# Transposed blocks of the third and fourth unit moved by pairs of tiles: one write and two reads in place of two writes and four reads

## The chip, the cores and the metric

The kernel runs on one core of one Trainium2 chip. The metric is the device time of one execution in microseconds; the time given is the median of several executions of the same program. A profile of one further execution is read here. Its engines are PE (TensorE matmul), PEld (TensorE's loading of weights, which runs beside PE), DVE (VectorE), ACT (ScalarE), POOL (GpSimd) and SP (SyncE, which here only issues DMAs). Every DMA of this kernel is issued by SP, in the order of its program.

## The reference

Chunked attention over 8 x 8 heads with sequences of 576 in chunks of 64, then a maxout layer with three weight matrices and an output projection:

```python
scores = scale * np.matmul(q_c, k_c.transpose(0, 1, 2, 4, 3))      # 64 x 64 for each head and chunk
scores = scores - np.max(scores, axis=-1, keepdims=True)
attn = np.exp(scores)
attn = attn / (np.sum(attn, axis=-1, keepdims=True) + 1e-09)
out = np.matmul(attn, v_c)
...
x = np.ascontiguousarray(attn_out.transpose(0, 2, 1, 3)).reshape(B * S, H * D)   # 4608 x 512
h = np.maximum(np.maximum(x @ w1, x @ w2), x @ w3)                               # 512 -> 768
return (h @ w_out).astype(np.float32)                                            # 768 -> 512
```

All of it is float32. A product of float32 operands is made on TensorE from three products of split operands (high and low part), so each step of the maxout layer is three matmuls, on lines 187, 188 and 189.

## The kernel before, in words

The 4608 rows are 36 tiles of 128 rows. The first 8 tiles form two plain groups of four. The other 28 form four "units" of 6, 8, 8 and 6 tiles (`UNITS`), for which the maxout layer is computed with fewer products from mixed operands. A unit runs nine "sets" of products, and then a projection. A set reads one mixed weight matrix from a ring of two places in on-chip memory. The ring is filled from DRAM in three parts for each set (line 557): two of 128 x 1536 elements (768 KB) and one of 128 x 512 (256 KB). The first part is needed by the first product of a set, the second part by the second product, the third part only during the next set. A product is six matmuls. In the third unit a matmul has 512 columns, in the fourth 384.

While the products of one unit run, the attention of the next unit's tiles is put between them, pair of tiles by pair of tiles. `insertion` gives each step of a pair a due time on an estimated clock, and `passed` issues every step whose time has come. So the order on each engine's queue is settled when the program is built. For one tile the steps are: load of q and k (line 225) and of v (229), scores S (237), maximum, subtraction, exponential, sum, reciprocal, normalisation on POOL (204), a transposition of the attention weights, and the products with the values, V (296). V of a pair stands on PE's queue just ahead of S of the pair after it.

The transposition differs by unit. In the first groups and the first two units it is made by PE and copied by ACT (`transpose`, `transposed`). In the third and fourth unit (`PAIR_D`; seven pairs) it is made of 32 x 32 blocks by DVE (`blocks`, line 270, tile `xs`), and the blocks are put in their places by a trip through DRAM: for each tile one write (`to_scratch`, line 274, 256 KB) and two reads of 64 partitions (`from_scratch`, line 279, 128 KB each) into the tile `e`. The due times are in `PAIR_D`: the blocks of the two tiles at 7.6 and 9.5, the writes at 8.4 and 10.3, the reads at 13.2 and 14.4. SP waits in its own program for whatever a DMA needs before it issues it: for the DVE's blocks ahead of a write, and for the landing of the write ahead of a read. Everything behind it on SP's queue waits too, the parts of the weight ring among it.

The buffers: `xs` is a pool of two places, `e` has two places by the parity of the tile.

Of the kernel before, what the change touches and what calls it, by code (L numbers as in the profile page):

```python
# [9 lines left out]
F32 = mybir.dt.float32  # L10
# [10 lines left out]
P = 128  # L21
# [9 lines left out]
PAIR = (("mx", 1.4, 2.9), ("sub", 2.2, 3.7), ("exp", 3.1, 4.6), ("sum", 4.1, 6.0), ("eps", 5.0, 6.9), ("rec", 5.2, 7.1),  # L31
        ("nrm", 5.6, 7.5))
PAIR_T = (("T", 10.8, 13.0, 0.46), ("at", 11.4, 13.7, 0.0))
PAIR_D = (("bt", 7.6, 9.5, 0.0), ("bw", 8.4, 10.3, 0.0), ("br", 13.2, 14.4, 0.0))
OUT = (1, 2, 6, 7, 5, 4, 3)
MIX = 0.5

# [26 lines left out]
def chunk_attn_maxout_kernel(  # L64
# [10 lines left out]
    nc = tc.nc  # L75
# [3 lines left out]
    pad = pad_p.tile([P, 224], F32, name="pad")  # L79
    cpool = ctx.enter_context(tc.tile_pool(name="cpool", bufs=1))  # L80
    att = ctx.enter_context(tc.tile_pool(name="att", bufs=1))
    xs_p = ctx.enter_context(tc.tile_pool(name="xs_p", bufs=2))
    ep = ctx.enter_context(tc.tile_pool(name="ep", bufs=1))
    ao_p = ctx.enter_context(tc.tile_pool(name="ao_p", bufs=1))
    stage_p = ctx.enter_context(tc.tile_pool(name="stage_p", bufs=1))
    dram = ctx.enter_context(tc.tile_pool(name="dram", bufs=1, space=bass.MemoryType.DRAM))
# [40 lines left out]
    for name in FIRST.split():  # L127
        k = (3 * int(name[1]) + int(name[2])) if name[0] in "WAXY" else None
# [79 lines left out]
    halves_of = [slice(0, 64), slice(64, 128)]  # L208
# [3 lines left out]
    def bank_of(name):  # L212
        if name not in banks_of:
            banks_of[name] = ps[name].tile([P, 2, 2, 4, 64], F32, name=name[-1])
        return banks_of[name]

    def plain_steps(t, x_of, col):


        st = {}  # L220
# [21 lines left out]
            nc.vector.tensor_reduce(out=st["mx"].rearrange("p (g c) -> p c g", c=2), in_=st["s"], axis=AX.X, op=ALU.max)  # L242

        def less():
            st["e"] = ep.tile([P, 4, 2, 64], F32, name="e", tag=("et", "e")[t % 2])
            most = st["mx"].rearrange("p (g c) -> p c g", c=2)
            nc.vector.tensor_tensor(out=st["e"].rearrange("p g c k -> p c g k"), in0=st["s"],  # L247
                                    in1=most.unsqueeze(3).broadcast_to([P, 2, 4, 64]), op=ALU.subtract)
# [12 lines left out]
                                    identity=ident)  # L261

        def transposed():
            st["at"] = xs_p.tile([P, 4, P], F32, name="xs")
            nc.scalar.copy(out=st["at"], in_=st["tp"])

        def blocks():
            st["b"] = xs_p.tile([P, 4, 4, 32], F32, name="xs")
            for c in range(2):
                nc.vector.transpose(out=st["b"][:, 2 * c:2 * c + 2], in_=st["e"][:, :, c].rearrange("p g (k two) -> p two g k", two=2))  # L270

        def to_scratch():
            st["d"] = dram.tile([2, P, 2 * P], F32, name=f"b{t}")
            nc.sync.dma_start(out=st["d"].rearrange("c p x -> p c x"), in_=st["b"].rearrange("p (c j) g x -> p c (j g x)", c=2))

        def from_scratch():
            st["at"] = ep.tile([P, 4, 4, 32], F32, name="e", tag=("et", "e")[t % 2])
            for c, rows in enumerate(halves_of):
                nc.sync.dma_start(out=st["at"][rows].rearrange("p i g x -> p i (g x)"),
                                  in_=st["d"][c].rearrange("(i k) (j x) -> (k j) i x", i=4, j=2))  # L280

        def moving(a, g, b):
            if "d" in st:
                return st["at"][a, b.start // 32:b.stop // 32, g, :]
            return st["at"][a, g, b]

        def values():
# [21 lines left out]
        def pair(both):  # L309
# [1 line left out]

        return dict(q=load_qk, v=load_v, pair=pair, S=scores, mx=maximum, sub=less, exp=exp, sum=total,
                    eps=lambda: st["guard"](), rec=lambda: st["invert"](), nrm=lambda *eng: st["norm"](*eng),
                    T=transpose, at=transposed, bt=blocks, bw=to_scratch, br=from_scratch, V=values, xh=high, xl=low)

    begun = {}

# [515 lines left out]
    def plan(at, pe, fn):  # L833
        heapq.heappush(due, (at, len(order), pe, fn))
        order.append(fn)
# [15 lines left out]
    def next_load(u, k):  # L851
# [6 lines left out]
        s=lambda: hold("s", lambda: late["hold"].tile([P, 5, HALF], F32, name="kept")),  # L858
# [3 lines left out]
    g = moe(starts[1], lambda: x_tiles(1))  # L862
# [5 lines left out]
    pairs = []  # L868
    for u, (_, t0, count) in enumerate(units):
        for n in range(0, count, 2):  # L870
            both = dict(col=n * P, norm=nc.gpsimd if u else nc.vector, turn=PAIR_D if u > 1 else PAIR_T)
            both["tiles"] = [begun[t] if t in begun else plain_steps(t, stage, (t - t0) * P) for t in (t0 + n, t0 + n + 1)]
# [17 lines left out]
    def insertion(when, k, behind=0.0, apart=1.0):  # L890

        scored = pairs[k]["tiles"] if k < len(pairs) else []
        if k:
            plan(when, 0.0, value_banks(pairs[k - 1]))
            for n, steps in enumerate(pairs[k - 1]["tiles"]):
                plan(when + 0.001 * (n + 1), 0.5, steps["V"])
                plan(when + 1.2 + 0.6 * n, 0.0, staged(pairs[k - 1], n))
        lead = 1.0 * bool(k)
        for n, steps in enumerate(scored):
            plan(when + 0.003 + 0.001 * n, 0.65, steps["S"])  # L900
            for name, *at in PAIR:
                fn = steps[name]
                plan(when + lead + at[n], 0.0, (lambda fn=fn: fn(pairs[k]["norm"])) if name == "nrm" else fn)
            for name, *at, pe in pairs[k]["turn"]:
                plan(when + lead + behind + at[n], pe, steps[name])
            plan(when + 6.0 + apart * n, 0.0, steps["v"])
        if k + 1 < len(pairs):
            for n, steps in enumerate(pairs[k + 1]["tiles"]):
                plan(when + 4.0 + apart * n, 0.0, steps["q"])
# [112 lines left out]
```

## Time and profile before

| | us |
|---|---|
| median of 3 runs | 608.79 (608.75 to 609.01) |
| profiled execution, its own time | 608.11 |
| its span, first instruction to last | 606.3 |
| PE busy | 598.4 (99% of the span) |
| DVE busy | 421.9 (70%) |
| ACT busy | 290.0 (48%) |
| POOL busy | 187.3 (31%) |
| DMA engines' mean share | 69.6% (the queue that carries the kernel's own DMAs) |

A matmul is pipelined: the next begins before it ends, so PE's busy time is not the sum of its instructions. "Idle before" of an instruction is the time its engine stood still ahead of it, with the instruction or DMA that ended the wait. The chain of waits starts from the last instruction and goes back to what released each step. For a DMA, "to landing" is the time from its issue on SP to the arrival of all its data. The pairs of the third unit have their V at 281.7, 305.7, 329.7 and 353.7 us, those of the fourth at 405.0, 439.8 and 474.7 us.

### The profile page before, as it was taken

What the parts mean: (1) busy time and instruction counts of PE and PEld (TensorE: products, weight loads), DVE (VectorE), ACT (ScalarE), POOL (GpSimd) and SP (SyncE); (2) the same over time, 40 slices, a digit from 0 to 9 for tenths busy, and PEclk for the clock granted to TensorE, in tenths of its full rate; (3) what the DMA queues carried; (4) which work ended last, traced back from release to release, by engine and by line L of the source; (5) the groups of instructions that cost most, each with busy time, mean ns of one, the idle gap of its engine ahead of it and who ended that gap; (6) DMA issues with size and microseconds to landing.
All of it is one profiled execution on the core that took longest, in us unless ns stands there. A gap on an engine that the chain in (4) does not pass through costs nothing.

```text
span 606.3 us, 12703 instructions
## 1 busy us (share of the span) xinstructions
PE 598.4 (99%) x5045; PEld 520.7 (86%) x5046; DVE 421.9 (70%) x700; ACT 290.0 (48%) x522; POOL 187.3 (31%) x168
## 2 busy tenths in 40 slices
PE   8899999999999999999999999999999999999997
PEld 4888878888899999998888888888888888999997
DVE  5898965767987986895664669936374587344373
ACT  4887634433454554555243345642333364433353
POOL 3422577877232424100250622002424000131300
PEclk9999999999999999999999999999999999999999
DMA  8988667755868998748886894468657444677532
GB/s 346 369 311 268 254 191 282 291 187 231 309 238 321 359 340 300 256 141 284 278 280 234 283 356 161 161 232 290 232 199 267 151 156 128 223 260 259 189 130 79
DMA packets 59483, 148.95 MB, mean 246 GB/s; under 512 B 5664, under 2 KB 24608, under 8 KB 59424
## 3 DMA queue, kind: packets, MB, share of 16 engines
q1 hardware_dynamic: 59424, 148.13, 69.6%
q8 instruction: 40, 0.66, 0.4%
q14 instruction: 19, 0.16, 0.1%
HBM read 116.92 MB, written 31.20 MB: 244 GB/s over the span
## 4 chain that ended last, share of the span: by engine, by line
PE 96%; DVE 2%; ACT 1%; issue 0%; DVEq 0%
PE pm L187 30%; PE pm L188 29%; PE pm L189 29%; PE s L237 3%; PE pm L296 3%; PE tp L260 1%; PE pm L795 1%; DVE e L247 0%; DVE sm L195 0%; DVE xl L307 0%; PE s L296 0%; DVE mx L242 0%; DVE sm L198 0%; ACT e L251 0%; DVE ao L172 0%
## 5 line engine op out<-in xcount | busy, mean ns | idle before, releaser
L187 PE MATMUL pm<-X,ring 128*128 128x512 f32 (+1 forms) x504 | 184.4, 366 | 0.0
L189 PE MATMUL pm<-X,ring 128*128 128x512 f32 (+1 forms) x504 | 182.4, 362 | 0.0
L188 PE MATMUL pm<-X,ring 128*128 128x512 f32 (+1 forms) x504 | 182.4, 362 | 0.0
L626 ACT COPY kept<-pm 128x384 f32<-128x384 f32 (+1 forms) x144 | 76.7, 534 | 153.0 <-PE pm L189 152.8
L187 PEld LDWEIGHTS pm<-X,ring 128*128 128x128 f32 x504 | 94.6, 188 | 10.8 <-ACT kept L626 0.4
L189 PEld LDWEIGHTS pm<-X,ring 128*128 128x128 f32 x504 | 94.6, 188 | 9.9
L188 PEld LDWEIGHTS pm<-X,ring 128*128 128x128 f32 x504 | 94.7, 188 | 9.7
L632 POOL TENSOR_TENSOR kept<-kept 128x384 f32<-128x384 f32 (+1 forms) x24 | 28.7, 1195 | 128.3 <-ACT kept L626 128.3
L629 DVE TENSOR_TENSOR pm<-pm,kept 128x384 f32<-128x384 f32 (+1 forms) x48 | 30.1, 628 | 50.8 <-PE pm L189 50.8
L187 PE MATMUL pm<-xh,wl 128*128 128x512 f32 (+1 forms) x156 | 60.1, 385 | 0.0
L188 PE MATMUL pm<-xl,wh 128*128 128x512 f32 (+1 forms) x156 | 58.4, 374 | 0.3 <-DVE xl L307 0.3
L189 PE MATMUL pm<-xh,wh 128*128 128x512 f32 (+1 forms) x156 | 58.3, 374 | 0.0
L594 DVE TENSOR_TENSOR H<-most,H 128x384 fp32r<-128x384 f32 (+1 forms) x72 | 48.7, 688 | 11.6 <-ACT H L591 11.3
L635 DVE TENSOR_TENSOR most<-pm,most 128x384 f32<-128x384 f32 (+1 forms) x72 | 44.5, 618 | 10.6 <-PE pm L189 9.4
L204 POOL TENSOR_TENSOR e<-e,sm 128x512 f32<-128x512 f32 x27 | 31.5, 1168 | 63.6 <-DVE sm L201 27.1
L632 POOL TENSOR_TENSOR most<-kept 128x384 f32<-128x384 f32 (+1 forms) x12 | 13.8, 1147 | 114.1 <-ACT kept L626 114.1
L528 DVE TENSOR_TENSOR X<-stage,X 128x768 fp32r<-128x768 f32 (+1 forms) x28 | 35.0, 1255 | 17.3 <-ACT X L524 17.1
L242 DVE TENSOR_REDUCE mx<-s 128x8 f32<-128x512 f32 x36 | 24.6, 684 | 32.1 <-PE s L237 31.9
L591 ACT CAST H<-most 128x384 fp32r<-128x384 f32 (+1 forms) x72 | 40.7, 569 | 10.5 <-PE pm L189 9.0
L251 ACT ACTIVATE e<-e 128x512 f32<-128x512 f32 x36 | 22.8, 632 | 27.4 <-DVE e L247 27.4
L188 PE MATMUL pm<-H,woh 128*128 128x384 f32 (+1 forms) x96 | 34.8, 363 | 0.0
L187 PE MATMUL pm<-H,wol 128*128 128x384 f32 (+1 forms) x96 | 34.7, 362 | 0.0
(119 smaller groups left out, 1051.1 us busy)
## 6 DMA issues: line engine op xcount, KB each, us to landing
ring<-w SPq DMA_DIRECT2D x72, 768.0 KB, 6.0
buf<-in_qk SPq DMA_DIRECT2D x36, 512.0 KB, 6.2
buf<-in_vb SPq DMA_DIRECT2D x36, 256.0 KB, 6.4
ring<-w SPq DMA_DIRECT2D x36, 256.0 KB, 4.0
w<-s SPq DMA_DIRECT2D x9, 768.0 KB, 3.8
out_x<-ao SPq DMA_DIRECT2D x24, 256.0 KB, 2.3
ring<-wo SPq DMA_DIRECT2D x8, 768.0 KB, 4.9
stage<-in_w SPq DMA_DIRECT2D x7, 512.0 KB, 6.3
```

Source lines behind the costliest of these rows:

```text
L187: nc.tensor.matmul(out=o, lhsT=al, rhs=bh, start=first, stop=False, skip_group_check=shared)
L188: nc.tensor.matmul(out=o, lhsT=ah, rhs=bl, start=False, stop=False, skip_group_check=shared)
L189: nc.tensor.matmul(out=o, lhsT=ah, rhs=bh, start=False, stop=last, skip_group_check=shared)
L204: eng.tensor_tensor(out=e, in0=e, in1=sm.unsqueeze(2).broadcast_to([P, 8, 64]), op=ALU.mult)
L242: nc.vector.tensor_reduce(out=st["mx"].rearrange("p (g c) -> p c g", c=2), in_=st["s"], axis=AX.X, op=ALU.max)
L528: return lambda: eng.tensor_tensor(out=X[i][:, 1], in0=source[i](), in1=X[i][:, 0].bitcast(F32), op=minus)
L591: nc.scalar.copy(out=H[i, jp][:, 0, :half], in_=hidden_block(i, jp))
L594: nc.vector.tensor_tensor(out=H[i, jp][:, 1, :half], in0=hidden_block(i, jp), in1=H[i, jp][:, 0, :half].bitcast(F32), op=minus)
L626: return lambda: nc.scalar.copy(out=to, in_=o)
L629: return lambda: nc.vector.tensor_tensor(out=o if w else M(jp, q), in0=o, in1=kept(k), op=plus)
L632: nc.gpsimd.tensor_tensor(out=kept(3) if w else M(jp, A22), in0=kept(3), in1=kept(p7), op=plus)
L635: return lambda: nc.vector.tensor_tensor(out=M(jp, q), in0=of, in1=M(jp, q), op=most)
```

## The change

The two buffers become one tile each, `exps` and `turned`, of 128 x 2 x 512 elements, of which each tile of a pair has a fixed half by its parity. In the plain groups and the first two units the halves are two runs of 512 elements. In the third and fourth unit the same memory is also seen as four rows of 2 x 128 (`exps_of_both`, `turned_of_both`), so that the blocks of both tiles stand side by side in runs of 256 elements. The DVE's blocks are written there with that stride. For each pair there is then one write of both tiles (due at 10.0) and two reads of 64 partitions (due at 13.9 and 14.3). The core of the diff:

```diff
-PAIR_D = (("bt", 7.6, 9.5, 0.0), ("bw", 8.4, 10.3, 0.0), ("br", 13.2, 14.4, 0.0))
+PAIR_D = (("bt", 7.6, 9.5, 0.0),)
+WRITE, READ = 10.0, 13.9
...
-    xs_p = ctx.enter_context(tc.tile_pool(name="xs_p", bufs=2))
+    xs_p = ctx.enter_context(tc.tile_pool(name="xs_p", bufs=1))
...
+    exps = ep.tile([P, 2, 512], F32, name="e")
+    turned = xs_p.tile([P, 2, 512], F32, name="xs")
+    exps_of_both, turned_of_both = (x.rearrange("p s x -> p (s x)").rearrange("p (i s x) -> p i s x", i=4, s=2)
+                                    for x in (exps, turned))
...
-            st["e"] = ep.tile([P, 4, 2, 64], F32, name="e", tag=("et", "e")[t % 2])
+            st["e"] = exps[:, t % 2].rearrange("p (g c k) -> p g c k", g=4, c=2)
...
-            st["at"] = xs_p.tile([P, 4, P], F32, name="xs")
+            st["at"] = turned[:, t % 2].rearrange("p (g x) -> p g x", g=4)
...
-            st["b"] = xs_p.tile([P, 4, 4, 32], F32, name="xs")
+            st["b"] = turned_of_both[:, :, t % 2].rearrange("p m (g x) -> p m g x", g=4)
...
-        def to_scratch():
-            st["d"] = dram.tile([2, P, 2 * P], F32, name=f"b{t}")
-            nc.sync.dma_start(out=st["d"].rearrange("c p x -> p c x"), in_=st["b"].rearrange("p (c j) g x -> p c (j g x)", c=2))
-
-        def from_scratch():
-            st["at"] = ep.tile([P, 4, 4, 32], F32, name="e", tag=("et", "e")[t % 2])
-            for c, rows in enumerate(halves_of):
-                nc.sync.dma_start(out=st["at"][rows].rearrange("p i g x -> p i (g x)"),
-                                  in_=st["d"][c].rearrange("(i k) (j x) -> (k j) i x", i=4, j=2))
...
+    def blocks_of_both(k):
+        st = {}
+
+        def write():
+            st["d"] = dram.tile([2, P, 512], F32, name=f"b{k}")
+            nc.sync.dma_start(out=st["d"].rearrange("c p x -> p c x"),
+                              in_=turned.rearrange("p s x -> p (s x)").rearrange("p (c x) -> p c x", c=2))
+
+        def read(c):
+            def fn():
+                nc.sync.dma_start(out=exps_of_both[halves_of[c]].rearrange("p i s x -> p i (s x)"),
+                                  in_=st["d"][c].rearrange("(i k) (j x) -> (k j) i x", i=4, j=2))
+            return fn
+
+        return (WRITE, write), (READ, read(0)), (READ + 0.4, read(1))
...
+        if scored and pairs[k]["turn"] is PAIR_D:
+            for at, fn in blocks_of_both(k):
+                plan(when + lead + behind + at, 0.0, fn)
```

On SP's queue, around the second pair of the third unit (loads of q, k, v, then the trip through DRAM; `b` is the place in DRAM, `ring<-w` a part of the weight ring), there stood before:

```order
L225 DMA buf<-in_qk 128x1024 x2
L229 DMA buf<-in_vb 128x512 x2
L274 DMA b_3709<-xs 128x2x256
L557 DMA ring<-w_1274 128x512
L274 DMA b_3729<-xs 128x2x256
L557 DMA ring<-w_1145 128x1536 x2
L279 DMA e<-b_3709 64x4x128 x2
L279 DMA e<-b_3729 64x4x128 x2
L557 DMA ring<-w_1145 128x512
```

and now:

```order
L231 DMA buf<-in_qk 128x1024 x2
L235 DMA buf<-in_vb 128x512 x2
L317 DMA b_3664<-xs 128x2x512
L569 DMA ring<-w_1260 128x512
L569 DMA ring<-w_1132 128x1536 x2
L322 DMA e<-b_3664 64x4x256 x2
L569 DMA ring<-w_1132 128x512
```

The first write is gone from its place ahead of the 256 KB ring part. The one write left stands ahead of that part, and it needs the blocks of both tiles, which only the second write needed before. The second pair of the fourth unit has the same pieces in the same order.

On the same queue, around the fourth pair of the third unit, there stood before:

```order
L274 DMA b_4234<-xs 128x2x256
L274 DMA b_4252<-xs 128x2x256
L279 DMA e<-b_4234 64x4x128 x2
L557 DMA ring<-w_1247 128x512
L557 DMA ring<-w_1055 128x1536
L279 DMA e<-b_4252 64x4x128 x2
L557 DMA ring<-w_1055 128x1536
```

and now:

```order
L317 DMA b_4172<-xs 128x2x512
L322 DMA e<-b_4172 64x4x256
L569 DMA ring<-w_1233 128x512
L569 DMA ring<-w_1043 128x1536
L322 DMA e<-b_4172 64x4x256
L569 DMA ring<-w_1043 128x1536
```

A read still stands on each side of the two ring parts, of the same bytes as the pair of reads that it replaces. What a read brings is different: before, the first two reads brought the whole of the first tile, now each brings half the partitions of both tiles, so that V of either tile needs both reads.

On every other engine the rows stand in the same order in both kernels; only the shape of the DVE's blocks is written differently (128x2x128 for 128x256).

## Rows read from the trace of the kernel before

**Rows 1.** The page's first part (busy time, share of the span, instructions of each engine) and its chain of waits by engine.

```profile
PE 598.4 (99%) x5045; PEld 520.7 (86%) x5046; DVE 421.9 (70%) x700; ACT 290.0 (48%) x522; POOL 187.3 (31%) x168
...
PE 96%; DVE 2%; ACT 1%; issue 0%; DVEq 0%
```

**Rows 2.** Busy time of each engine from 255 to 480 us, the stretch in which the seven pairs are worked on: stretch, length, then busy us and instructions of PE, PEld, DVE, ACT and POOL, the granted clock of TensorE, the DMA engines' mean share, GB/s.

```profile
255.00:480.00 225.00, 224.96 (x1782) 188.75 (x1781) 147.10 (x244) 96.36 (x166) 52.10 (x41) 1.00 0.71 239
```

**Rows 3.** What PE's loading of weights waited for from 255 to 480 us: us in total, times, longest.

```profile
PEld pm L296 <- issue: 2.1, 6, 0.4
PEld pm L188 <- DVE H L594: 0.4, 1, 0.4
```

**Rows 4.** DMA issues by line: tile, count, KB each, median us from issue to landing.

```profile
w<-s SPq DMA_DIRECT2D x9, 768.0 KB, 3.8
...
b<-xs SPq DMA_DIRECT2D x14, 256.0 KB, 2.6
e<-b SPq DMA_DIRECT2D x28, 128.0 KB, 3.1
```

**Rows 5.** All instructions of the reads' line and of the blocks' line: count, duration in ns (least, median, most), first and last start.

```profile
L279 SPq DMA_DIRECT2D e<-b x28: 573/607/873, 259.4 to 455.3; - x28
...
L270 DVE STREAM_TRANSPOSE xs<-e x28: 392/404/445, 254.3 to 451.7; 128x256 f32<-128x256 f32 x28
```

**Rows 6.** SP's instructions in order of time (start, us from the first to the end of the last, line, tile, count): around the second pair of the third unit, the fourth pair of the third unit, and the second pair of the fourth unit.

```profile
290.90 0.38 SPq L274 DMA_DIRECT2D b<-xs  x1
291.38 0.41 SPq L557 DMA_DIRECT2D ring<-w  x1
292.75 0.37 SPq L274 DMA_DIRECT2D b<-xs  x1
293.21 0.92 SPq L557 DMA_DIRECT2D ring<-w  x2
...
340.14 2.65 SPq L274 DMA_DIRECT2D b<-xs  x2
344.52 1.24 SPq L279 DMA_DIRECT2D e<-b  x2
345.87 1.02 SPq L557 DMA_DIRECT2D ring<-w  x2
346.99 1.24 SPq L279 DMA_DIRECT2D e<-b  x2
...
414.15 0.38 SPq L274 DMA_DIRECT2D b<-xs  x1
...
416.01 0.37 SPq L274 DMA_DIRECT2D b<-xs  x1
```

**Rows 7.** Single DMAs by line with the time to landing, each in a stretch so short that it holds this one alone: the second 768 KB part of the ring behind the second pair of the third unit; the second write and the last read of that unit's fourth pair; the second 768 KB part of the ring behind the second pair of the fourth unit.

```profile
L557 SPq DMA_DIRECT2D ring<-w x1: 407/407/407, 293.7 to 293.7; - x1
...
DMA to landing us min/median/max: 7.1/7.1/7.1
...
L274 SPq DMA_DIRECT2D b<-xs x1: 370/370/370, 342.4 to 342.4; - x1
...
DMA to landing us min/median/max: 2.6/2.6/2.6
...
L279 SPq DMA_DIRECT2D e<-b x1: 607/607/607, 347.6 to 347.6; - x1
...
DMA to landing us min/median/max: 5.1/5.1/5.1
...
L557 SPq DMA_DIRECT2D ring<-w x1: 391/391/391, 417.0 to 417.0; - x1
...
DMA to landing us min/median/max: 7.2/7.2/7.2
```

**Rows 8.** PE and PEld in order of time, one instruction each (the bracket is the idle time before it, and what ended it): a matmul's weights that wait for DVE; the first weights taken from the ring part that landed after 293.7 (those of the seventh matmul of its set); V of the fourth pair of the third unit; the first weights from the ring part issued at 417.0.

```profile
270.01 0.19 PEld L188 LDWEIGHTS pm<-H,woh 128*128 128x128 f32 x1 [0.37 <-DVE H L594]
...
302.68 0.19 PEld L187 LDWEIGHTS pm<-X,ring 128*128 128x128 f32 x1
...
353.74 1.16 PE L296 MATMUL pm<-e,buf 64*64 64x64 f32 x64
...
425.94 0.19 PEld L187 LDWEIGHTS pm<-X,ring 128*128 128x128 f32 x1
```

**Rows 9.** Short stretches, with the columns of rows 2; the last two are the DMA engines' mean share and GB/s.

```profile
291.00:292.00 1.00, 1.00 (x6) 0.83 (x5) 1.00 (x3) 0.00 (x0) 0.00 (x0) 1.00 0.17 60
292.00:293.00 1.00, 1.00 (x6) 0.81 (x5) 1.00 (x4) 0.59 (x1) 0.06 (x1) 1.00 1.02 238
...
293.98:300.85 6.87, 6.87 (x32) 5.68 (x31) 3.10 (x5) 1.42 (x3) 0.26 (x1) 1.00 1.06 324
...
343.00:344.00 1.00, 1.00 (x6) 0.84 (x5) 1.00 (x2) 0.00 (x0) 1.00 (x1) 1.00 0.78 278
344.00:345.00 1.00, 1.00 (x6) 0.84 (x5) 0.18 (x1) 0.59 (x1) 1.00 (x2) 1.00 0.16 47
...
347.00:348.00 1.00, 1.00 (x7) 0.81 (x6) 0.00 (x0) 0.59 (x1) 0.21 (x1) 1.00 1.07 215
...
349.00:350.00 1.00, 1.00 (x6) 0.83 (x5) 0.00 (x0) 0.23 (x2) 0.00 (x0) 1.00 0.99 387
```

More of the change, by code (lines that the diff above doesn't have):

```diff
@@ L263, in transposed @@
         def transposed():
-            st["at"] = xs_p.tile([P, 4, P], F32, name="xs")
+            st["at"] = turned[:, t % 2].rearrange("p (g x) -> p g x", g=4)
             nc.scalar.copy(out=st["at"], in_=st["tp"])
         def blocks():
-            st["b"] = xs_p.tile([P, 4, 4, 32], F32, name="xs")
+            st["b"] = turned_of_both[:, :, t % 2].rearrange("p m (g x) -> p m g x", g=4)
             for c in range(2):
                 nc.vector.transpose(out=st["b"][:, 2 * c:2 * c + 2], in_=st["e"][:, :, c].rearrange("p g (k two) -> p two g k", two=2))
-        def to_scratch():
-            st["d"] = dram.tile([2, P, 2 * P], F32, name=f"b{t}")
-            nc.sync.dma_start(out=st["d"].rearrange("c p x -> p c x"), in_=st["b"].rearrange("p (c j) g x -> p c (j g x)", c=2))
-        def from_scratch():
-            st["at"] = ep.tile([P, 4, 4, 32], F32, name="e", tag=("et", "e")[t % 2])
-            for c, rows in enumerate(halves_of):
-                nc.sync.dma_start(out=st["at"][rows].rearrange("p i g x -> p i (g x)"),
-                                  in_=st["d"][c].rearrange("(i k) (j x) -> (k j) i x", i=4, j=2))
         def moving(a, g, b):
-            if "d" in st:
-                return st["at"][a, b.start // 32:b.stop // 32, g, :]
+            if "b" in st:
+                return exps_of_both[a, b.start // 32:b.stop // 32, t % 2, 32 * g:32 * g + 32]
             return st["at"][a, g, b]
@@ L313, in plain_steps @@
                     eps=lambda: st["guard"](), rec=lambda: st["invert"](), nrm=lambda *eng: st["norm"](*eng),
-                    T=transpose, at=transposed, bt=blocks, bw=to_scratch, br=from_scratch, V=values, xh=high, xl=low)
+                    T=transpose, at=transposed, bt=blocks, V=values, xh=high, xl=low)
+    def blocks_of_both(k):
[10 more added lines that the diff above has]
+        return (WRITE, write), (READ, read(0)), (READ + 0.4, read(1))
     begun = {}
```

## The prediction

> **What bounds the kernel now.** I read the page's first part and its chain of waits first, because they say which engine a change must touch. PE is busy 99% of the span, and 96% of the chain that ends last runs on PE [rows 1]. That share is a mean over the whole kernel, so the second view was the stretch in which the change acts, from 255 to 480 us: of 225.00 us PE is busy 224.96, at a granted clock of 1.00 [rows 2]. The third view, what PE's loading of weights waited for there, names no DMA: 2.1 us are "issue" ahead of V, six times, and 0.4 us are a wait for DVE [rows 3], at 270.01 us [rows 8]. So the trip through DRAM costs the kernel nothing today, as long as its results and the weight ring arrive before PE wants them. What can move the time is a place where an arrival that was early comes late. The last view was therefore SP's queue around each pair, with the landings [rows 6, 7], held against PE's first use [rows 8].
>
> **The sum in advance.** The terms are made against the profiled execution: 608.11 us, of which 606.3 are the span and 1.8 lie around it. Its time is 0.68 below the median of the runs, 608.79; a change of the profile is carried over to the median unchanged.
>
> **What is removed, and what hides it.** The seven pairs lose 14 writes and 28 reads [rows 4] and gain 7 writes and 14 reads of twice the size. The bytes are the same. On SP a read takes 0.61 us to issue [rows 5] and a write 0.37 [rows 6]; 14 x 0.61 + 7 x 0.37 = 11.1 us of issuing go, 1.6 us for each pair. All of it lies beside PE's work, so it counts as 0. If it were to count at all, it could only be through PE's waits in that stretch, which are 225.00 - 224.96 = 0.04 us of PE standing still and the 0.4 us for DVE. A gain is thus at most 0.4 us. The "issue" time ahead of V is no such reserve: V still comes after matmuls of another shape, with the same 64 products.
>
> **DVE's blocks.** The 28 block transpositions stay; they write runs of 128 elements with a stride. The trace has no such form. The lower bound is the same duration; for the upper I take the spread of the form that is there, 445 against 404 ns [rows 5], 0.04 us each. Only the first pair's four stand ahead of the place where PE waits for DVE, so the price is 0 to 0.16 us. I take 0: the elements and the 32 x 32 pieces are the same. Elsewhere DVE is busy 147.10 of 225 us [rows 2], which covers it.
>
> **The write that now waits for both tiles.** This is the added wait. SP issues the one write when the second tile's blocks are done, which is when the second write was issued before; what stands behind it on SP is the weight ring and, later, the reads. Three places have little room.
>
> (a) Second pair of the third unit. The first write left SP at 290.90, the second at 292.75 [rows 6]. The 256 KB ring part between them can wait; the second 768 KB part behind them can't: issued at 293.7, it landed 7.1 us later, at 300.85, and PE loads weights from it at 302.68 [rows 7, 8]. The room is 1.83 us. If the whole shift of 292.75 - 290.90 = 1.85 us is passed on, PE stands 0.02 us. If the DMA engines make it up, the landing moves less. They were nearly idle (share 0.17) in the us before the first write's data began to flow at 292 [rows 9], 1.1 us after its issue; now they begin at about 293.85. Until the part has landed they carry 512 + 256 + 2 x 768 KB = 2.36 MB. At the 324 GB/s of the busy stretch [rows 9] that takes 7.3 us and ends at 301.1; at the mean rate over the same bytes before, 2.36 MB in 300.85 - 292.0 = 8.85 us, it ends at 302.7. I take the middle, 301.9: no wait.
>
> (b) Second pair of the fourth unit, the same order on SP: shift 416.01 - 414.15 = 1.86 us; the part issued at 417.0 landed 7.2 us later, at 424.2, for weights at 425.94 [rows 6 to 8]. The room is 1.76 us; passed on whole, PE stands 0.1 us, and with the engines catching up as in (a), 0.
>
> (c) Fourth pair of the third unit. V starts at 353.74, and the last read landed at 347.6 + 5.1 = 352.7 [rows 7, 8]: 1.0 us of room. The second write left SP at 342.4 and landed 2.6 us later [rows 7]; the first read followed the first write's landing at 344.52 [rows 6]. Now the read follows the landing of 512 KB issued at 342.4. The trace has no such write; the nearest rows are 256 KB at 2.6 us and a 768 KB write at 3.8 [rows 4], so 2.6 to 3.8, and I take 3.3 (both halves start together, where the first had a head start; one more half at the 278 GB/s of 343 to 344 [rows 9] is 0.9 us). The first read is issued at 345.7 instead of 344.5, 1.2 us late (0.5 to 1.7). Behind it SP has two reads instead of four, which gives back 0.61 us ahead of the two ring parts, and the DMA engines were all but idle from 344 to 345 (share 0.16), so bytes are not the limit there. The last read then lands 0.6 (0 to 1.7) late: at 353.3, between 352.7 and 354.4. V stands 0, at worst 0.7 us.
>
> One thing could bring the reads forward. From 347 to 348, when reads in runs of 512 bytes flowed, the DMA engines moved 215 GB/s, and 387 from 349 to 350, when the ring's longer rows did [rows 9]; at full share both times. In runs of 1 KB, 256 KB (0.26 MB) may take as little as 0.26 / 0.387 = 0.7 us instead of 0.26 / 0.215 = 1.2, and the last read would land 0.5 us sooner, at 352.8. I leave that out of the sum, and let it count against late reads. [...]
>
> The other four pairs count 0: of all landings that I compared, those of (a) to (c) have the least room. How the rest stand is seen in the last pair: its last read leaves SP at 455.3 [rows 5], and its V starts at 474.7.
>
> **What stays.** The first groups and the first two units get fixed halves in place of two rotating places, with the same tile in the same half. The change's rows show no other order there. Price 0.
>
> **Sum.** SP's issuing 0, blocks 0, (a) 0, (b) 0, (c) 0: 608.1 for a profiled execution, 608.8 for the median. By the bounds: -0.4 at the best, and 0.16 + 0.02 + 0.1 + 0.7 = 1.0 at the worst.
>
> **Rivals.**
>
> Slower: the trip becomes the bound at the late places. The mechanism is SP's one queue: a write that waits for both tiles, then a read that waits for the whole write, holds back ring parts and reads, and PE stands for them. For it speaks that the room is 1.0 to 1.8 us, about as large as the shifts; against it, that SP gets 0.61 us back at each pair and the DMA engines have gaps. It decides from a shift of 1.0 us in the last read of (c), or 1.8 in (a). If the whole shift is passed on and the larger write also holds the DMA engines for 3.8 - 2.6 = 1.2 us more [rows 4], PE stands 0.02 + 1.2 in (a), 0.1 + 1.2 in (b) and 0.7 in (c), 3.2 us: 612.0. A milder form, 0.3 to 1.0 us at one place alone, is likelier: 609.1 to 609.8.
>
> Faster: the shorter queue lets ring parts be issued earlier, and PE's small stalls go. It can give back at most the 0.4 us above: 608.4. For it speaks the 11.1 us of issuing that goes; against it, that PE waits for no DMA.
>
> It doesn't do what it says: the two halves of one tile are taken for one buffer in the first groups, and a tile waits there for its neighbour. The chain's 2% on DVE and 1% on ACT lie mostly in that beginning, where PE covers little. If there one tile's copy or subtraction had to wait for its neighbour's V, half of the 1.16 us that V of two tiles takes [rows 8], for four pairs, the time would be 608.8 + 4 x 0.58 = 611.1. Against it: on no engine does an instruction move there, and the halves are separate runs of memory.
>
> **How the numbers follow.** A measurement of this kernel tells about 0.2% (1.2 us) from no change. Forecast, nothing visible (608.8, own range 608.3 to 609.3): 0.78. Small gain to 608.4: 0.10, nearly all of it within 0.2%. Late reads or ring parts: 0.10, of which half stay under 1.2 us. Coupled halves: 0.02. So within 0.2%: 0.89; slower by more: 0.05 + 0.02, less a little, 0.06; faster by more, by something that I don't see in the trace: 0.05. The range goes from the gain's bound with some spread of the runs, 608.2, to the worst sum of the bounds, 608.8 + 1.0 = 609.8.
>
> **What the profile of the changed kernel would show.** Right: PE busy over 224.9 of the 225 us from 255 to 480, no DMA among what PEld waited for, V of the fourth pair at its old distance from the products before it; SP's writes as 7 of 512 KB landing in about 3.3 us, its reads as 14 of 256 KB. (a) right: the second 768 KB part lands at 301.1 to 302.7. Wrong: PEld waiting at V or at a set's seventh matmul for a read or the ring; or any row of the first 250 us that starts later than before.

## The result, and the profile after

The changed kernel takes 614.09 us (median of 9 runs, 610.79 to 617.10), the kernel before, on the same chip, 609.31 (9 runs, 608.75 to 611.08): a ratio over all these runs of 1.0069, 95% interval 1.0051 to 1.0087 (the medians alone give 1.0078). It is 0.7% slower; the forecast was no change, and 614.09 lies outside its range of 608.2 to 609.8. In six of the nine runs the mean granted clock was 0.996 or 0.997 and not 1.0, which is part of the loss (below).

The profiled execution took 613.4 us. Its page's first part and its chain, against [rows 1]; then PE's busy time from 255 to 480 us, against [rows 2] (the row is the sum of two stretches), and what PE waited for there (us in total, times, longest):

```profile
PE 599.2 (98%) x5045; PEld 520.8 (85%) x5046; DVE 422.3 (69%) x700; ACT 290.0 (47%) x522; POOL 187.0 (31%) x168
...
PE 93%; DMA 3%; DVE 2%; ACT 1%; issue 0%; DVEq 0%
```

```profile
sum 225.00, PE 222.02 PEld 186.11 DVE 147.46 ACT 94.07 POOL 50.46; mean PE 111.01 PEld 93.06 DVE 73.73 ACT 47.04 POOL 25.23
```

```profile
PE pm L292 <- DMA e<-b: 2.3, 1, 2.3
PE pm L188 <- DMA ring<-w: 0.7, 1, 0.7
```

DMA is in the chain now, with 3% (the flights of two DMAs, 9.1 us each, that PE waited for), and PE stands for 3.0 us in this stretch where it stood for 0.04. Two waits make that up: one of V (L292) for a read, one of a product (L188) for the ring. The span grew by 5.0 us, though, from 606.3 to 611.3 us. Another 1.4 of it come earlier: against the kernel before, PE is 0.5 us late from a V at 23.9 us on and 0.9 us more from a product at 189.0 on. At both it sat idle, and the profile names nothing that it waited for (`issue`):

```profile
PE pm L190 <- issue: 0.7, 1, 0.7
PE x L292 <- issue: 0.4, 1, 0.4
```

The profile of e0 below, the same kernel again, has neither of these two; that of e12 has the second one and the time of before. So nothing shows that the change makes them.

The long wait is place (c), the fourth pair of the third unit. SP there, against [rows 6], and the two reads' time to landing, against [rows 7]:

```profile
343.90 0.37 SPq L317 DMA_DIRECT2D b<-xs  x1
346.69 0.59 SPq L322 DMA_DIRECT2D e<-b  x1
347.36 1.03 SPq L569 DMA_DIRECT2D ring<-w  x2
348.44 0.58 SPq L322 DMA_DIRECT2D e<-b  x1
```

```profile
L322 SPq DMA_DIRECT2D e<-b x1: 586/586/586, 346.7 to 346.7; - x1
...
DMA to landing us min/median/max: 3.8/3.8/3.8
...
L322 SPq DMA_DIRECT2D e<-b x1: 585/585/585, 348.4 to 348.4; - x1
...
DMA to landing us min/median/max: 9.1/9.1/9.1
```

And PE in order of time, against V in [rows 8]:

```profile
355.11 0.32 PE L292 MATMUL pm<-e,buf 64*64 64x64 f32 x2
357.69 0.99 PE L292 MATMUL pm<-e,buf 64*64 64x64 f32 x53 [2.26 <-DMA e<-b]
...
359.71 0.50 PE L188 MATMUL pm<-X,ring 128*128 128x512 f32 x1
```

V begins at 355.11 with two matmuls, and PE is idle for 2.26 us until the second read has landed, 9.1 us after its issue; the last read of before took 5.1. Seen from V's start, that read was issued 6.7 us ahead (348.44 against 355.11), sooner than before (347.6 against 353.74, 6.1): it is not issued late, it is under way for long.

What the DMA engines did while it flew, in stretches of 2 us from some 1.5 us after the last read's issue, in the kernel before and in the changed one (columns of rows 2):

```profile
349.00:351.00 2.00, 2.00 (x11) 1.65 (x10) 0.00 (x0) 0.59 (x2) 0.00 (x0) 1.00 0.97 359
351.00:353.00 2.00, 2.00 (x11) 1.65 (x10) 1.76 (x3) 0.00 (x0) 0.00 (x0) 1.00 1.09 353
```

```profile
350.00:352.00 2.00, 2.00 (x10) 1.65 (x9) 0.00 (x0) 0.96 (x2) 0.00 (x0) 1.00 0.92 325
352.00:354.00 2.00, 2.00 (x11) 1.65 (x10) 1.40 (x3) 0.00 (x0) 0.00 (x0) 1.00 0.94 211
354.00:356.00 2.00, 1.44 (x8) 0.83 (x6) 1.32 (x2) 0.59 (x1) 0.07 (x1) 1.00 1.04 251
```

From 350 to 352 us they move 325 GB/s. Then, for 4 us, their share is as full as before, but they move 211 and 251 GB/s instead of 359 and 353.

### The profile page after: what moved, and what is told of

Its sections match the earlier page's. It is cut to its first block, busy times and chain, and to the rows that moved or that the text cites. A ratio compares the mean times of both kernels' runs of the same rounds, so it can differ in the third digit from the quotient of the medians.

```text
span 611.3 us, 12659 instructions
## 1 busy us (share of the span) xinstructions
PE 599.2 (98%) x5045; PEld 520.8 (85%) x5046; DVE 422.3 (69%) x700; ACT 290.0 (47%) x522; POOL 187.0 (31%) x168
## 4 chain that ended last, share of the span: by engine, by line
PE 93%; DMA 3%; DVE 2%; ACT 1%; issue 0%; DVEq 0%
PE pm L188 29%; PE pm L189 28%; PE pm L190 28%; PE s L243 3%; PE pm L292 3%; DMA ring<-w 1%; DMA e<-b 1%; PE tp L266 1%; PE pm L807 1%; DVE e L253 0%; DVE sm L196 0%; DVE xl L303 0%; PE s L292 0%; DVE mx L248 0%; DVE sm L199 0%
## 5 line engine op out<-in xcount | busy, mean ns | idle before, releaser
L188 PE MATMUL pm<-X,ring 128*128 128x512 f32 (+1 forms) x504 | 184.4, 366 | 0.7 <-DMA ring<-w 0.7
L188 PEld LDWEIGHTS pm<-X,ring 128*128 128x128 f32 x504 | 94.6, 188 | 11.7 <-issue 1.1
L188 PE MATMUL pm<-xh,wl 128*128 128x512 f32 (+1 forms) x156 | 60.0, 385 | 0.0
L188 PE MATMUL pm<-H,wol 128*128 128x384 f32 (+1 forms) x96 | 34.7, 362 | 0.0
```

The costliest lines, as they stand in the source:

```text
L188: nc.tensor.matmul(out=o, lhsT=al, rhs=bh, start=first, stop=False, skip_group_check=shared)
```

## Experiments

The theories, by the letters that the expectations use. A: each read now fills one half of the partitions, for both tiles, and one half alone among ring parts is slow. B: the one write waits for both tiles and makes everything behind it on SP late. C: V of either tile now needs both reads, where the first tile needed only the early ones. D: runs of 1 KB are slow. P: what counts is how many ring parts stand ahead of the last read. None of the kernels leaves out computation.

All results in one table. A ratio is against the kernel before on the same chip, whose median was 609.31 us beside the changed kernel and 608.80 to 608.89 beside the others. "Ahead": the ring parts issued between the first and the last read of (c). "Landed": when the last read landed, us from V's start, negative where it was early. "V stands": the longest gap between two starts in V, or ahead of it. In e13 and e14, where V itself begins late, both are counted from 0.32 us after the start of the product ahead of it, which is where V begins in the others. "Rate": what the DMA engines moved from 1.5 us after the last read's issue to its landing. The last four columns are of one profiled execution each.

| kernel | median us | ratio, 95% interval | ahead, KB | flight us | landed | V stands | rate GB/s |
|---|---|---|---|---|---|---|---|
| before | 608.8 | 1 | 256+768 | 5.1 | -1.0 | 0 | 354 |
| changed | 614.09 | 1.0051-1.0087 | 256+768 | 9.1 | +2.4 | 2.5 | 281 |
| e0 changed, again | 612.20 | 1.0040-1.0088 | 256+768 | 8.6 | +1.9 | 1.9 | 287 |
| e1 reads together | 609.52 | 1.0004-1.0028 | none | 3.8 | -2.8 | 0 | |
| e12 256 KB between | 608.94 | 0.9993-1.0017 | 256 | 4.4 | -2.5 | 0 | |
| e7 both later | 609.72 | 1.0009-1.0029 | none | 3.7 | -1.9 | 0 | |
| e4 before, late writes | 608.84 | 0.9992-1.0009 | 256+768 | 5.6 | -0.6 | 0 | 346 |
| e10 early writes, reads together | 609.69 | 1.0003-1.0023 | none | 3.8 | -3.3 | 0 | |
| e6 before, halves apart | 611.51 | 1.0029-1.0078 | 256+2x768 | 7.4 | +2.2 | 1.7 | 322 |
| e9 before, second tile later | 610.30 | 1.0010-1.0033 | 256+2x768 | 6.7 | +0.8 | 0.3 | 346 |
| e14 before, first tile later | 610.84 | 1.0019-1.0048 | 256+2x768 | 6.8 | +1.9 | 1.6 | 364 |
| e2 four reads by tile | 609.88 | 1.0004-1.0025 | 256+768 | 5.4 | +0.5 | 0 | 344 |
| e13 as e2, tiles swapped | 610.98 | 1.0020-1.0042 | 256+768 | 6.5 | +1.2 | 0.9 | 324 |
| e11 halves apart, by tile | 610.62 | 1.0020-1.0047 | 256+768 | 6.4 | +1.6 | 1.1 | 303 |
| e8 both halves, by columns | 612.51 | 1.0056-1.0083 | 256+768 | 6.9 | +3.3 | 3.3 | 318 |

**Is (c) the place?** e0 is the changed kernel again. e1, e12 and e7 leave everything as it is but the order at (c):

```
-        return (WRITE, write), (READ, read(0)), (READ + 0.4, read(1))
+        return (WRITE, write), (READ, read(0)), (READ, read(1))           # e1
+        return (WRITE, write), (READ, read(0)), (READ + 0.2, read(1))     # e12
+        return (WRITE, write), (READ + 0.4, read(0)), (READ + 0.4, read(1))   # e7
```

> The changed kernel as it is, a second profile and a time beside the other kernels of this set. If the slow second read of the fourth pair of the third unit is the cause (theory A), V stands there 1.5 to 3 us again, and the ratio is 1.004 to 1.009; the 0.84 us stall of the fourth unit (b) may be there or not, since the kernel with the two reads together has the same order there and did not show it. If the cause is spread over many places (rival), the profile shows other stalls in other places and V here stands under 1 us.

> The changed kernel with the two reads of a pair planned at one time, so that they are issued one behind the other in every pair; the only pair where this moves anything is the fourth of the third unit, where two parts of the ring stood between them. Theory A (the second read, alone between ring parts and into one half of the partitions, is slow and slows the ring parts around it): V of that pair stands less than 0.7 us instead of 2.47, the ring parts there land within 8 us, and the kernel comes to 610.5 to 612 us, with the 0.84 us stall in the fourth unit (b) left. Theory B (the single write, which waits for both tiles, makes everything behind it on SP late): the reads here still wait for the same landing of the write, so V stands 1.5 to 3 us and the time stays at 613 to 614.5. Theory C (each tile needs both reads): as A, since the second read is earlier.

> The changed kernel with the second read planned 0.2 earlier, so that in the fourth pair of the third unit only the 256 KB ring part stands between the two reads and the 768 KB part comes behind both. Theory A (a half alone among ring parts): it still takes 6.5 us or more, V stands 0.3 us or more, 610 to 612. Rival P (position behind the 768 KB part): it lands within 5 us of its issue, V does not stand, 609 to 610.

> The changed kernel with the first read of a pair moved to the second's place: in the fourth pair of the third unit both reads are issued directly behind each other, behind the write, a 256 KB and a 768 KB ring part. Theory A (alone and into one half): together they land within 7 us of their issue although as late as the slow one was, V stands 0 to 1 us, 609 to 611. Rival (what stands ahead of the read in the queue makes it late): both land 8 to 10 us after their issue, V stands 2 us or more, 612 to 615.

e0 lost the same again, 1.0064, with V standing 1.9 us at the same place. In e1 the two reads stand together, V runs without a gap, and 1.0016 is left; the stall at (b) that A's range of 610.5 to 612 us counted on did not come. In e12 the 256 KB part is still between them, only the 768 KB part has gone behind; SP's rows there and the second read:

```profile
345.83 0.58 SPq L322 DMA_DIRECT2D e<-b  x1
346.50 0.56 SPq L569 DMA_DIRECT2D ring<-w  x1
347.11 0.59 SPq L322 DMA_DIRECT2D e<-b  x1
347.79 1.50 SPq L569 DMA_DIRECT2D ring<-w  x3
```

```profile
L322 SPq DMA_DIRECT2D e<-b x1: 586/586/586, 347.1 to 347.1; - x1
...
DMA to landing us min/median/max: 4.4/4.4/4.4
```

It lands after 4.4 us and the time is the time of before, 1.0005. So (c) is the place, one 768 KB part ahead of the second read is what makes it late, and nothing else in the change costs anything that these runs tell for certain. A's 6.5 us or more for a half among ring parts fell here: the 256 KB ring part between the reads did no harm. e7 did not test what it was meant to: its ring parts were issued while SP would have waited for the write, some 4 us ahead of the reads, and most of their data had moved when the reads' data began to flow (the engines' share was 0.50 and 0.35 in the us from 347 and from 348); both reads landed within 3.7 us.

**Is it the late write?** e4 and e6 start from the kernel before. e4 plans the two writes at the time of the one; e10 goes the other way, from e1, and writes each tile's blocks early.

```
-PAIR_D = (("bt", 7.6, 9.5, 0.0), ("bw", 8.4, 10.3, 0.0), ("br", 13.2, 14.4, 0.0))
+PAIR_D = (("bt", 7.6, 9.5, 0.0), ("bw", 9.99, 10.0, 0.0), ("br", 13.2, 14.4, 0.0))   # e4
-        return (WRITE, write), (READ, read(0)), (READ, read(1))
+        return (8.4, write(0)), (10.3, write(1)), (READ, read(0)), (READ, read(1))    # e10
```

> The kernel before with both writes of a pair planned together at the time of the changed kernel's one write (10.0), so that SP waits for the second tile's blocks at the same place and the ring parts behind it are as late as after the change; two writes of 256 KB and four reads of 128 KB are left as they were. Theory B: ring parts at (a) and (b) come 1.2 to 1.9 us later, a stall of 0.5 to 1 us appears in (b), and the kernel takes 610 to 612 us. Theory A: the writes' time costs nothing by itself, 608.8 to 609.8, no stall over 0.3 us in (b).

> The changed kernel with each tile's blocks written as soon as they are there (two writes of 128 KB a tile, at the times of before) and the two reads of a pair issued one behind the other. If what is left over in e1 (0.16 per cent) comes from the one late write (theory B, the ring parts at (a) and (b) issued 0.75 us closer to their use), the lead of these parts is 9 us or more again and the kernel takes 608.4 to 609.2, ratio 0.999 to 1.001. If it comes from the runs of 1 KB and reads of 256 KB, 609.3 to 610 is left.

e4 takes the time of before, 1.0001. But the trace shows that it did only a part of what it was meant to do. Its first write leaves SP when it did before (290.66 us, against 290.90 in [rows 6]):

```profile
290.66 2.23 SPq L274 DMA_DIRECT2D b<-xs  x2
292.98 1.40 SPq L557 DMA_DIRECT2D ring<-w  x3
```

What it makes late is the ring parts, the second 768 KB part at (a) by 0.5 us against PE's work, where the change makes it late by 0.75. That these 0.5 us cost nothing is shown; that the late write costs nothing is shown by e12, which has the one write as the changed kernel has it, and the time of before. Theory B falls by both together. e10 does not get the rest of e1 back (1.0013), so that rest is not the late write either.

**On the kernel before.** e6 does one thing of the change alone: in (c) the second tile's two halves are read on two sides of a ring part. e9 puts both halves behind both 768 KB parts, directly behind each other; e14 is e9 with the first tile late in place of the second.

```
-... ("br", 13.2, 14.4, 0.0))
+... ("r0", 13.2, 14.4, 0.0), ("r1", 13.8, 15.0, 0.0))   # e6: a read for each half
+... ("br", 13.2, 15.0, 0.0))                            # e9
+... ("br", 15.0, 13.2, 0.0))                            # e14
```

> The kernel before with nothing of the change but this: in the fourth pair of the third unit the second tile's two reads (128 KB, one for each half of the partitions) are issued on two sides of a 768 KB ring part, where they stood directly behind each other. Theory A (a half read alone among ring parts is slow and slows them): the last read takes 7 us or more to land, packets of the ring around it take over 300 ns, V's second tile stands 0.5 to 2 us, 609.5 to 611. Rival (only the position behind the ring counts): it lands within 6 us of its issue, no stall over 0.3 us, 608.6 to 609.4.

> The kernel before with both reads of the second tile (128 KB each, both halves of the partitions, directly behind each other) planned 0.6 later, so that in the fourth pair of the third unit they come behind two 768 KB ring parts, one more than before and as many as stood ahead of the last read of e6. Theory A (a read into one half alone is slow, position is not): the last read lands within 6.5 us of its issue, the DMA moves 340 GB/s or more during its flight, V's second tile stands under 0.5 us, 608.7 to 609.6. Rival P (it is the position: what is queued ahead on the one queue makes the last read late, whatever half it fills): it lands 7 us or more after its issue, V's second tile stands 1 to 2 us as in e6, 610.5 to 612.

> The kernel before with the places of e9 (one tile's two reads behind both 768 KB ring parts), but it is the first tile that is read late and the second early. Theory C: the last read lands 0.8 us behind V's start as in e9, V's first tile stands 0.7 to 1.2 us where its second stood 0.26, and the kernel takes 610.8 to 612, more than e9's 610.3. If the need does not matter: as e9, 609.8 to 610.7.

V of e6, of e9 and of e14 on PE, in order of time:

```profile
353.36 0.79 PE L299 MATMUL pm<-e,buf 64*64 64x64 f32 x34
355.60 0.63 PE L299 MATMUL pm<-e,buf 64*64 64x64 f32 x27 [1.45 <-DMA e<-b]
```

```profile
354.13 1.47 PE L296 MATMUL pm<-e,buf 64*64 64x64 f32 x61
```

```profile
355.02 0.29 PE L296 MATMUL pm<-e,buf 64*64 64x64 f32 x2 [1.49 <-DMA e<-b]
355.48 1.10 PE L296 MATMUL pm<-e,buf 64*64 64x64 f32 x59 [0.17 <-DMA e<-b]
```

With the same parts ahead, the halves apart lose 0.54% and the halves together 0.22%. Against V's start, e6's last read lands 1.4 us later than e9's; half of that is its later issue (5.2 us ahead of V, not 5.9), half its longer flight, 7.4 against 6.7 us. So one more 768 KB part ahead costs by itself (P), 0.22% in e9. That the half apart costs more (A) is not shown: the 0.7 us of flight are less than the 1.1 us by which e2 and e13 differ below, with the same DMAs, and e6's loss holds 0.6 us for which a product in the fourth unit stood for the ring in its profile, and the lower clock of four of its runs (below). e14 shows C: what is late is needed first, and V stands 1.5 us ahead of its first matmul and 0.2 ahead of its third, instead of for 0.3 us in its middle. e6 took more than the 611 us that A allowed it, and e9 lies between the two ranges that were written down for it.

**The shape of the reads.** These keep the change's write and the two ring parts ahead of the last read. e2 reads tile by tile; e13 is e2 with the tiles swapped; e11 reads the first half of both tiles, then the second, a read for each tile; e8 reads both halves each time, half of the columns of both tiles, in runs of 1 KB.

```
+            for c in range(2):                                     # e2, e13: both halves of tile s
+                nc.sync.dma_start(out=exps_of_both[halves_of[c]][:, :, s], ...
+            for s in range(2):                                     # e11: half c of either tile
+                nc.sync.dma_start(out=exps_of_both[halves_of[c]][:, :, s], ...
+            for c in range(2):                                     # e8: both halves, columns n
+                nc.sync.dma_start(out=exps_of_both[halves_of[c], 2 * n:2 * n + 2]...
```

> The changed kernel with its one write, but with four reads of a pair as before the change: each tile's two halves directly behind each other (128 KB each, runs of 512 bytes), the second tile's after the two ring parts. Theory A: no half is read alone, so V in the fourth pair of the third unit stands under 0.7 us, and the reads of (b) land in 6 to 8 us; the time is 609 to 610.5. Theory B (the one write): the ring parts and reads behind the write are as late as in the changed kernel; the stall of 0.8 us in (b) stays, V stands 1 us or more, 611.5 to 614. Theory C (a tile needs both reads): V's first tile starts in time, 609.5 to 611.

> The kernel of e2 (one write; four reads of 128 KB, both halves of a tile directly behind each other) with the tiles' reads swapped: the second tile's come first, and the first tile's, which V needs first, stand behind the 256 KB and the 768 KB ring part. The DMAs have the shape and the places of e2. Theory C (what V needs first is now what is read last): V stands 0.4 to 1 us, since the last read of e2 landed 0.5 us behind V's start, and the kernel takes 610.3 to 611.5. If the need does not matter and only the shape of the reads does (A, D): V stands under 0.2 us, 609.4 to 610.2 as e2.

> The changed kernel with each read of 256 KB into one half of the partitions cut into two of 128 KB, one for each tile, with runs of 512 bytes; the order stays as in the changed kernel: first half of both tiles, two ring parts, second half of both tiles. If it is the half alone or the need for all reads (theories A and C), V stands 1.5 us or more again and the time is 611.5 to 614; if it is the runs of 1 KB (theory D), V stands under 1 us and the time is 609 to 610.5.

> The changed kernel with its one write and runs of 1 KB, but with each of the two reads replaced by two of 128 KB, one for each half of the partitions, of half the columns: what is read before and behind the two ring parts goes into all 128 partitions both times. Theory A: the last reads land within 6.5 us of their issue, V stands 0 to 0.7 us, 609 to 610.5. Theory C (that V needs what is read last, whatever its shape): last landing 8 to 10 us after its issue, V stands 1.5 us or more, 611.5 to 614.

V of e2 and of e13:

```profile
355.28 1.18 PE L292 MATMUL pm<-e,buf 64*64 64x64 f32 x61
```

```profile
354.26 1.52 PE L292 MATMUL pm<-e,buf 64*64 64x64 f32 x61 [0.80 <-DMA e<-b]
```

e13 against e2 changes the need alone (C): the same DMAs, and 1.0031 instead of 1.0015, V standing 0.9 us. In e2 a last read that landed 0.5 us behind V's start made nothing stand. Not all of the 0.9 is the need, though: e13's last read also flew 1.1 us longer in its profile. e11 needs the last read as the changed kernel does, but in runs of 512 bytes: V stands 1.1 us, 0.34%, between the two ranges that were written down for it. e8 went against A: with both halves each time it still lost 0.69%, all four reads being needed by V's first tile. Its write took 4.4 us to land, so its last read left 3.6 us ahead of V; a second reason beside C, and one that I can't explain. The same write landed in 2.7 us in the changed kernel's two profiles and in 2.7 to 3.9 in e1, e2, e11, e12 and e13. The rates of the last column are lowest where a half is read in runs of 1 KB, 281 and 287; the others, 303 to 364, overlap.

**A read over all partitions.** e5 was to take the halves away altogether:

> The changed kernel with its one write and with runs of 1 KB, but with every read spread over all 128 partitions (four reads of 128 KB, one for each quarter of the columns; two before the two ring parts in the fourth pair of the third unit and two behind them). Theory A (what is slow is a read into one half of the partitions alone): the last read there lands within 5 us of its issue, V stands under 0.7 us, and the time is 609 to 611. Theory C or D (that both reads are needed; that runs of 1 KB are slower): V still waits for the last read, 7 us or more after its issue, and the time stays at 612 to 614. Theory B: the 0.84 us stall in (b) stays.

It took 655.95 us, 1.0782 (1.0741 to 1.0822): a miss for every theory. In (c), with nothing else under way but its reads, and what PE waited for from 255 to 520 us:

```profile
340.00:342.00 2.00, 2.00 (x10) 1.68 (x9) 0.69 (x1) 0.93 (x2) 0.40 (x1) 1.00 0.13 48
342.00:344.00 2.00, 2.00 (x10) 1.65 (x10) 0.69 (x1) 0.17 (x1) 0.00 (x0) 1.00 0.14 48
```

```profile
PE pm L292 <- DMA e<-b: 21.6, 5, 8.1
PE pm L188 <- DMA ring<-w: 10.3, 2, 6.5
```

The share is 0.13 of 16 engines, 2.1 engines' worth, and they move 48 GB/s. The outermost dimension of that read's source has two entries, the halves. That the one comes from the other is a guess of mine, which no other run tests.

## Why the prediction was wrong

**What bounds the kernel.** Right: PE waits for no DMA before, and what moves the time is an arrival that comes late. The places were the right three, and (c) the worst.

**SP's issuing, and DVE's blocks, at 0.** Right: e12 has all of both and the time of before. The view of [rows 3] has a second wait of 0.4 us for DVE, ahead of a V, that the bound on the gain left out; no gain came of either. DVE is busy 147.46 us in the stretch, 147.10 before [rows 2].

**(a) and (b), no wait.** Nearly. The second 768 KB part at (a) landed after 7.4 us, at 303.3, which is 301.9 without the 1.4 us by which this profile is late from its beginning: the time in the sum. In e0 it landed after 8.6 us, and PE waited 0.2 us for it. At (b) it took 9.1 us instead of 7.2 [rows 7] in the first profile, and PE stood 0.7 us, against a worst case of 0.1; in e0, e1, e7 and e12 it stood 0.3 us at most.

**(c), the step that failed.** "The last read then lands 0.6 (0 to 1.7) late: at 353.3 ... V stands 0, at worst 0.7 us." The sum took the shift of the write and kept the read's own 5.1 us. The shift had the wrong sign. The write landed in 2.7 us and not 3.3 (its range over all profiles, 2.7 to 4.4, holds both), and the sum gave back the 0.61 us of one read on SP where two are gone ahead of the last read, one on each side of the ring parts: from the first read to the last SP took 1.75 us (346.69 to 348.44), and 3.1 before (344.52 to 347.6). So the last read was issued 0.6 us sooner against V than before. The flight was the term that was mis-sized: 9.1 and 8.6 us. The read landed 1.9 to 2.4 us behind V's start, and V, whose first tile had not needed it before, stood 1.9 to 2.5.

**The 215 GB/s.** I read the stretch from 347 to 348 [rows 9] as the price of runs of 512 bytes. Its packets, counted by size, say otherwise. Here are those of that stretch, and those of e1 from 349.4 to 350.0, where the same rate comes back (how many are under 512 bytes, under 2 KB, under 8 KB):

```profile
DMA packets 222, 0.21 MB, mean 215 GB/s; under 512 B 16, under 2 KB 151, under 8 KB 222
```

```profile
DMA packets 64, 0.13 MB, mean 215 GB/s; under 512 B 1, under 2 KB 1, under 8 KB 64
```

In the first, 135 packets are the reads' and carry 0.07 MB; the 71 larger ones, two thirds of the bytes, are rows of 2 KB, which only the ring's 256 KB part has there. In the second no packet of a read is left at all. So the 215 GB/s is no price of the reads' runs, and the 215 against 387, which I let count against late reads, was no evidence that runs of 1 KB flow faster. The 0.5 us that longer runs were to give back never came.

What one half of the partitions alone makes is seen where nearly all packets are the reads': in the first profile the first read from 348.5 to 349.0 (148 of 151 packets are under 2 KB); in e1, where the two reads stand together, both and then the second alone:

```profile
348.50:349.00 0.50, 0.50 (x4) 0.42 (x3) 0.00 (x0) 0.50 (x1) 0.45 (x1) 1.00 0.93 311
```

```profile
347.80:348.40 0.60, 0.60 (x4) 0.51 (x3) 0.00 (x0) 0.51 (x1) 0.00 (x0) 1.00 1.09 362
348.50:349.20 0.70, 0.70 (x5) 0.58 (x4) 0.00 (x0) 0.12 (x1) 0.00 (x0) 1.00 1.11 272
```

That the second read flows alone from 348.5 is inferred from the landings (349.2 and 350.2 us). One half alone makes 272 and 311 GB/s here, both together 362: 14 to 25% less. By these rows the change, which makes one read of a half out of two, had a price, and I had no rival for it. How much of the long flight is this price is not shown.

**The clock.** It was in no sum. In e0 V stood for 1.7 us of idle time, and then:

```profile
356.00:357.00 1.00, 0.78 (x47) 0.81 (x51) 0.00 (x0) 0.00 (x0) 0.28 (x1) 0.92 1.10 451
357.00:360.00 3.00, 3.00 (x92) 2.79 (x87) 0.53 (x1) 1.07 (x2) 0.00 (x0) 0.50 1.03 417
360.00:361.00 1.00, 1.00 (x5) 0.85 (x4) 1.00 (x3) 0.00 (x0) 0.00 (x0) 0.87 0.91 303
```

```profile
356.23 1.39 PE L292 MATMUL pm<-e,buf 64*64 64x64 f32 x59 [1.70 <-DMA e<-b]
...
360.33 0.40 PE L190 MATMUL pm<-X,ring 128*128 128x512 f32 x1
```

The granted clock fell to 0.50 until 360. From V's second start to that product took 4.10 us, and 2.59 where the clock stayed at 1.00 (357.69 to 360.28 in the first profile): 1.5 us on top of the 1.9. e6's eight runs fall in two groups: four with mean clock 1.0 took 609.5 to 610.6 us, four with 0.994 to 0.997 took 612.4 to 614.9. The changed kernel's three runs at 1.0 took 610.8 to 613.4, its other six 613.4 to 617.1. So these two kernels, whose V stood 1.7 and 2.5 us in a profile, took 0.7 to 4.1 us more than the median of before in the runs at 1.0, and 3.6 to 7.8 us more in those with the lower clock. It is no rule: in e8, with a stall of 3.3 us, two runs at 0.994 and 0.997 took 612.2 and 613.0, and three at 1.0 took 612.25 to 612.92.

**The rivals.** The slower one had the side right and the mechanism wrong: it was priced as SP's queue held back by the write, 612.0 at the extreme, and e12 shows that the one write costs nothing that can be told. The gain was not seen. That two halves of one tile are taken for one buffer is ruled out by e12, which has them. One sign of being wrong did come, rows of the first 250 us that start later, by 1.4 us in the first profile; it is not this rival, since e0 and e1 have the same halves there and not these waits.

**What stays open.** How the 3.5 us by which the last read moved against V divide between the half, the runs and what differs from execution to execution: the profiles of e2 and e13, with the same DMAs at (c), differ by 1.1 us in the last read's flight. And the 0.1 to 0.2% left in e1, e2, e7 and e10, for which neither the late write nor runs of 1 KB is the cause; e12 has it within its interval or not at all. In e1 and e7 a part of it lies outside the span: a run's time less its span is 2.1 to 2.2 us in the changed kernel, e0, e1, e7 and e12, which all have the change's one write and two reads, 1.9 in e10 and 1.8 before; 0.35 us, or 0.06%, for which no row gives a reason.

## What to carry to other kernels

When two small transfers become one, look at what each piece now covers: whether it reaches all partitions (one half alone made 272 and 311 GB/s here, both together 362), whether its first user needs all of it (e2 and e13, with the same DMAs, 1.0015 and 1.0031), and what stands ahead of it on the queue (e12 and the changed kernel, 1.0005 and 1.0069). Here a read of 256 KB that had to arrive in time belonged ahead of a 768 KB prefetch and not behind it: moving that one read by one place in the queue gave back the whole loss. Room is the landing against the first use, and the flight of a read behind 1 MB of other traffic is not a constant to be copied from the trace of before: 5.1 us there, 9.1 and 8.6 in the changed kernel. And a rate in a short stretch belongs to the packets that flow in it, as the 215 GB/s of which two thirds were the ring's: count them by size before it is laid to one DMA.

## What was not expected of the hardware

- While a 256 KB read into one half of the partitions and 768 KB ring parts were under way together, the DMA engines moved 211 GB/s at a share of 0.94 (changed kernel, 352 to 354 us), against 359 at 0.97 with the 128 KB reads of before. One half alone was read at 272 to 311 GB/s, both halves together at 362 (first profile, e1).
- Reads over all 128 partitions, whose source has an outermost dimension of two, ran at a share of 0.13 to 0.14 of the 16 DMA engines, at 48 GB/s; PE stood 21.6 us for them, and 10.3 us for ring parts (e5).
- After V's stall of 1.7 us idle the granted clock went to 0.50 for over 3 us in e0; after one of 2.26 us in the first profile it did not.
